# Input weights of a dense layer decoded ahead and parked in memory, with one scale to four chunks, and two transfers of a crossing issued in one step

## The chip, the cores and the metric

The kernel runs on one core of one Trainium2 chip. The metric is the device time of one execution in microseconds, from three runs of the kernel before; a separate profiled execution gives the trace. The engines are called TensorE (PE in the rows, PEld for its weight loads), VectorE (DVE), ScalarE (ACT), GpSimd (POOL) and SyncE (SP, here a queue of DMA issues).

## The reference, cut to what matters

```python
x = attention(q, k, v, w_pre, w_post)   # talking heads, 4 x 12 heads, 448 tokens, 64 wide
x = x.reshape(1792, 768)
a, b = x @ w1, x @ w2                    # 768 -> 1024
x = ((a * b) @ w3) @ w_out               # 1024 -> 1024 -> 768
h = x @ w_in                             # 768 -> 2048   (the input layer)
r = np.maximum(h, 0.0)
return (r * r) @ w_out2                  # 2048 -> 768   (the last stage)
```

All data is float32 in the reference; the weights arrive as float64 words, of which the kernel makes fp32 on the chip ("decode").

## The kernel before

Every fp32 factor is held as two fp16 halves, high and low, and each product is three matmuls (high x high, high x low, low x high). Halves need a common power of two as scale, which needs the largest magnitude over all 128 partitions. That is found by a *crossing*: a column of per-partition sums is stored to memory (`across`, L833), read back broadcast to all partitions (`ac`, L837), and reduced on DVE (`largest_sent`, L852), all DMAs issued from POOL; `pow2` (L109 to L114) makes the scale.

The work goes in stages: attention (to about 455 us); the first dense layer (columns `fc` 0 to 7, 144 matmuls each, `hidden_tile`); the product of `w3` and `w_out` into `M` (680 to 750); the x2 stage, `h @ M` over four strips of 448 tokens (750 to 860), each strip with a crossing of its own (`x2_steps`) before its halves are cast; the input layer (`layer_in`, eight pairs `p` of 128 output columns, 144 matmuls a pair, `in_tile`), whose results are squared on ACT (L1595, L1596) and stored (`g`); and the last stage, a product by a seven-multiplication scheme (L1715), whose weights `ow` are mixed from pairs of decoded output weights (`mixed_out`).

Weights come in *chunks* of 768 KB, in the order of the list `chunks`. One chunk's decode is ACT `Abs` (L799), DVE L800, L804, L807, ACT `Abs` with a sum (L811) and DVE L813. For `w1`, `w2` and `in`, two chunks make a pair: both are decoded, their sums `tot` cross together, and both are cast, the high half on ACT (L904), the low half on DVE (L907) (`pair_steps`). While the crossing is away, `between` decodes the chunk that follows if its kind allows it. An output chunk (`out`) is decoded and parked in memory as fp32 (`kept_out`), to be read again by `mixed_out`. Decoded chunks are in a ring of three tiles (`xa`), raw ones in a ring of two, cast weights in two rings of four (`w_tile`). The list after `M` is: in 0, in 1, out 0 to 7, in 2, in 3, out 8, out 9, in 4, in 5, and so on to out 15, then in 10 to in 15.

The order of instructions on the engines is written out while the program is built, by a planner. It has a clock `now`, which `tick` moves on as matmuls are written (1.13 for each two contraction steps, six matmuls), expected busy times of ACT, DVE and POOL, and streams of steps, each with an engine, a cost or a rest. A step is written when its engine is expected free within `ahead` and its rests are over; `GATE` holds a chunk until `allow[0]` has reached it. Where a result is asked for that is not written yet (`need`), its stream's steps are written at once, without rests. Streams cost nothing on the chip; they only place instructions in the engines' in-order queues. The lines on the crossing's wait in `pair_steps` are

```python
WAY = 14.0
...
yield REST, lambda: max(0.0, box["at"] + WAY + 3.0 - now[0]), None
yield DVE, 1.0, scale
...
yield REST, HAND, None
for k, z in ((0, 0), (1, 0), (0, 1), (1, 1)):
    yield (ACT, DVE)[z], 1.0, lambda k=k, z=z: cast(k, z)
```

In the x2 stage `allow[0]` is the place of out 7; in pair `p` of the input layer it is the place of in `2p + 3`.

Of the kernel before, what the change touches and what calls it, by code (L numbers as in the profile page):

```python
# [10 lines left out]
F32 = mybir.dt.float32  # L11
# [7 lines left out]
P = 128  # L19
# [16 lines left out]
def talking_heads_attention_moe_moe2(  # L36
# [675 lines left out]
            chunks += [("wl", f) for f in range(NFC // 2, NFC)]  # L712
        chunks.append(("w3", 4 * p + 2 * j + g))
    OG = NF2 // 2
    for p in range(NP2):
        chunks += [("in", 2 * p), ("in", 2 * p + 1)]
        if p == 0:
            chunks += [("out", j) for j in range(OG)]
        elif 2 * p + OG <= NF2:
            chunks += [("out", OG + 2 * p - 2), ("out", OG + 2 * p - 1)]  # L720
    place = {c: i for i, c in enumerate(chunks)}
    kept = {j: dram.tile([P, DM], F32, name=f"kept_{j}") for j in range(NFC // 2, NFC)}
    kept_out = [dram.tile([P, DM], F32, name=f"kept_out_{j}") for j in range(NF2)]
    out_sums = [sm.tile([P, OG], F32, tag="osum", name="osum", bufs=2) for _ in range(2)]
    wraw, wsp = {}, {}
# [97 lines left out]
    ncross = [0]  # L823
    ACT, DVE, POOL, REST, GATE = range(5)

    def crossing(src, n, box, wait):

        ncross[0] += 1
        d = dram.tile([P, n], F32, name=f"across_{ncross[0]}")
        w = 2 if n < 3 else n  # L830

        def there():
            nc.gpsimd.dma_start(d, src)  # L833

        def back():
            t = sm.tile([P, P * w], F32, tag=f"ac{w}", name="ac", bufs=4 // w)[:, : P * n]
            nc.gpsimd.dma_start(  # L837
                t, d.rearrange("p n -> (p n)").unsqueeze(0).to_broadcast([P, P * n])
            )
            box["sent"] = t  # L840

        yield after(wait)
        yield REST, 0.7, None
        yield POOL, 0, there
        yield REST, WAY / 2, None
        yield POOL, 0, back
        yield REST, WAY / 2, None
# [14 lines left out]
    def pair_steps(i, dma, between=None):  # L862
# [5 lines left out]
        n = 2  # L868

        def issue():  # L870
            box["way"] = Stream(crossing(tot, 2, box, ACT))
            streams.append(box["way"])
            box["at"] = now[0]

        def scale():
            finish(box["way"])
            box["scale"] = pow2(largest_sent(box.pop("sent"), n), 14, "ws", n)

        def turned():
# [53 lines left out]
        if between:  # L933
            yield from between(i + 2)
        if dma is not None:
            yield REST, lambda: max(0.0, box["at"] + WAY + 3.0 - now[0]), None
            yield DVE, 1.0, scale
        yield REST, HAND, None
        for k, z in ((0, 0), (1, 0), (0, 1), (1, 1)):
# [3 lines left out]

    def between(i):

        if i >= len(chunks) or chunks[i][0] not in ("wo", "in", "out", "w1") or i > allow[0]:
            return
        if chunks[i][0] == "out":
            return
        if chunks[i][0] == "wo":  # L950
            yield from one_steps(i)
            begun[i] = True
            return
        t1 = sm.tile([P, 1], F32, tag="t1", name="t1")
        load_to(i + 1)
        x, ops = decode(wraw.pop(i), DM, t1)

        def hand(total):
            nc.vector.tensor_copy(total, t1)
            return x  # L960

        yield from read_raw(i, x, ops)
        begun[i] = hand

    def one_steps(i):
        kind, j = chunks[i]
        load_to(i + 1)
        t = wraw.pop(i)
        if kind == "wl":
            load_to(i + 2)  # L970
            hh = wo_tiles(j)[0]
            yield ACT, 0.9, lambda: nc.scalar.copy(hh, t.bitcast(F32))

            def low():
                nc.vector.tensor_tensor(t, t.bitcast(F32), hh, op=ALU.subtract)
                wsp["wo", j] = wsp[chunks[i]] = (hh, t)

            yield DVE, 1.0, low
            return
        n = 4 * P if kind == "w3" else DM  # L980
        if kind == "out":
            x, ops = decode(t, n, out_sums[j // OG][:, j % OG : j % OG + 1])
            yield from read_raw(i, x, ops)
            yield POOL, 0, lambda: put_later(DVE, ("kept", j // OG), kept_out[j], x)
            wsp[kind, j] = True
            return
        x, ops = (decode_alone if kind == "w3" else decode)(t, n)
        yield from read_raw(i, x, ops)
        if kind == "w3":
            hh, ll = (  # L990
                pools["w"].tile([P, 4 * P], F32R, tag="wv"[z], name="w3", bufs=WB) for z in range(2)
            )
        elif j >= NFC // 2:
            yield POOL, 0, lambda: nc.sync.dma_start(kept[j], x)
            return
        else:
            hh, ll = wo_tiles(j)
        yield ACT, 0.9 * n / DM, lambda: nc.scalar.copy(hh, x)

        def low():  # L1000
            nc.gpsimd.tensor_tensor(ll, x, hh, op=ALU.subtract)
            wsp[kind, j] = (hh, ll)

        yield POOL, 2.0, low

    def load_to(n):
        while done[0] < min(n, limit[0]):
# [38 lines left out]

    def weight_steps(i):
        while i < len(chunks):
            if chunks[i][0] in ("w1", "in"):
                yield GATE, i + 1, None  # L1050
                yield from pair_steps(i, nc.gpsimd, between)
                i += 2
            else:
                if begun.pop(i, None) is None:
                    yield GATE, i, None
                    yield from one_steps(i)
                i += 1
# [13 lines left out]
                puts.remove(x)  # L1071

    def flush_kept():
        for g in range(2):
            flush(("kept", g))

    def tick(us, act=0.0, dve=0.0):
        flush(None, now[0])
# [10 lines left out]
    def finish(st):  # L1089
        while st.step(True) is not None:  # L1090
            pass
        if st in streams:
            streams.remove(st)
# [365 lines left out]
    xb = [sp.tile([P, NDC, NT], F16, tag="S", name="x2") for _ in range(2)]  # L1459
    x2 = [(xb[0][:, c], xb[1][:, c]) for c in range(NDC)]  # L1460

    allow[0] = place["out", OG - 1]

    def x2_steps(i, ts, xm):
        box = {}
# [10 lines left out]

    x2_done = []
    for i in range(B):
        xm = sm.tile([P, NDC + 1], F32, tag="xm", name="xm")
        ts = []  # L1480
        for c in range(NDC):
# [28 lines left out]
    def mixed_out(g):  # L1510
# [10 lines left out]

        def sides(q):
            bs = [w_tile(1, "ob").rearrange("p a d -> p (a d)").bitcast(F32) for _ in range(2)]
            flush(("kept", g))
            for z in range(2):
                nc.sync.dma_start(bs[z], kept_out[g * OG + 2 * q + z])
            box["b"] = bs
# [45 lines left out]
        return mixed[g]  # L1573

    def layer_in(p, gm):
        ws = [need(("in", 2 * p + j)) for j in range(2)]
        for st in x2_done[: B - 1]:
            finish(st)
        sc = [sm.tile([P, B], F32, tag=f"sci{j}", name="sci") for j in range(2)]
# [107 lines left out]

    gm = None
    for p in range(NP2):
        allow[0] = place["in", 2 * p + 3] if 2 * p + 4 < NF2 else len(chunks)  # L1690
        g, r = divmod(2 * p, OG)
        if r == 0:
            gm = sm.tile([P, OG, B], F32, tag="gm", name="gm")
        layer_in(p, gm)
        if r == OG - 2:
            g_scales[g] = Stream(g_scale(g, gm))
            streams.insert(0, g_scales[g])
        if p == 0:
            streams.append(mixed_out(0))
        elif p == NP2 - 1:  # L1700
            streams.append(mixed_out(1))
        if p == NP2 - 2:
            streams.append(tokens)
# [179 lines left out]
```

## Time and profile before

| | |
|---|---|
| median of three runs | 1371.28 us (1371.28 to 1372.92) |
| the profiled execution's own time | 1368.81 us |
| its span in the trace | 1367.0 us |
| mean granted TensorE clock | 0.969 |
| busy share PE, DVE, ACT, POOL | 92%, 68%, 56%, 39% |

The busy share is an average over stages. The granted clock is given as a share of 2.4 GHz. In a row of the timeline the brackets hold the engine's idle time before the instruction and what ended it.

### The profile page before, as it was taken

The numbers are of one execution on the slowest core, as the hardware profiler recorded it, in microseconds if no ns is written. First come the engines' busy times: TensorE is split into PE (matmuls) and PEld (weight loads), VectorE is DVE, ScalarE is ACT, GpSimd is POOL, SyncE is SP. The second block draws the span as 40 slices with busy tenths as digits, with TensorE's granted clock in tenths as the row PEclk, the third lists the DMA queues.
The fourth block names the chain that finished last, engine by engine and source line by source line (L and its number), as shares of the span: only waits on it lengthen the run. The fifth ranks groups of instructions, "written<-read, shape, count | busy, mean of one in ns | idle before, by whom it ended". The sixth has DMA issues, their size and how long they took to land. (4 is left out here: it accounts for less than half of the span.)

```text
span 1367.0 us, 26049 instructions
## 1 busy us (share of the span) xinstructions
PE 1254.2 (92%) x10022; PEld 760.5 (56%) x10022; DVE 932.2 (68%) x1758; ACT 759.5 (56%) x1502; POOL 531.3 (39%) x545
## 2 busy tenths in 40 slices
PE   8999999999999999888999999876586899999998
PEld 4666766766666555444599555432242344555565
DVE  6988898888898566655797565444653323699764
ACT  6878888788876344333443444445554545665330
POOL 4997788897794010000122000001400003577340
PEclk9999999999999999988999999998888999999999
DMA  6455455455567233232343245356735533555562
GB/s 190 131 159 154 131 158 153 125 162 157 141 173 205 53 104 89 74 85 85 105 150 108 51 79 168 66 110 188 217 109 145 133 106 123 177 157 184 158 198 93
DMA packets 130336, 182.99 MB, mean 134 GB/s; under 512 B 33348, under 2 KB 110788, under 8 KB 130212
## 3 DMA queue, kind: packets, MB, share of 16 engines
q1 hardware_dynamic: 125364, 176.41, 46.1%
q0 software_dynamic: 1712, 2.51, 1.3%
q10 hardware_dynamic: 3136, 2.40, 0.7%
q8 instruction: 79, 1.29, 0.4%
q14 instruction: 45, 0.37, 0.1%
HBM read 104.37 MB, written 38.38 MB: 104 GB/s over the span
## 5 line engine op out<-in xcount | busy, mean ns | idle before, releaser
L1106 PE MATMUL mm<-x,w 128*128 128x448 f16 x2196 | 437.8, 362 | 91.3 <-ACT w L904 72.3
L1106 PEld LDWEIGHTS <-w 128*128 128x128 f16 x2304 | 227.3, 100 | 320.5 <-ACT w L904 76.7
L1715 PE MATMUL mm<-ow,ao 128*128 128x384 f16 x1176 | 192.4, 326 | 6.1 <-DVE st L1731 5.6
L285 PE MATMUL p<-Bt,wpre_k 120*120 120x448 f32 x360 | 159.4, 560 | 5.1 <-DMA Bt<-S 4.9
L1715 PEld LDWEIGHTS <-ao 128*128 128x128 f16 x1176 | 115.0, 98 | 83.4 <-issue 7.7
L381 PEld LDWEIGHTS <-EH 120*112 120x112 f16 (+1 forms) x1440 | 124.7, 130 | 45.0 <-issue 37.2
L403 DVE TENSOR_TENSOR ATl<-o,ATh 112x480 f16<-112x480 f32 x180 | 116.1, 645 | 25.3 <-ACT ATh L397 24.6
L354 POOL TENSOR_SCALAR EH<-E,st 120x448 f16<-120x448 f32 (+1 forms) x152 | 115.7, 769 | 43.7 <-DVE st L337 32.7
L307 ACT ACTIVATE E<-p,st 120x448 f32<-120x448 f32 x180 | 116.1, 645 | 22.9 <-DVE st L299 13.6
L381 PE MATMUL o<-wph,EH 120*112 120x120 f16 x720 | 123.9, 219 | 1.8 <-DVE ATl L403 0.9
L397 ACT CAST ATh<-o 112x480 f16<-112x480 f32 x180 | 101.2, 562 | 43.1 <-PE o L381 38.1
L381 PE MATMUL o<-wph,EL 120*112 120x120 f16 x720 | 122.0, 216 | 0.0
L381 PE MATMUL o<-wpl,EH 120*112 120x120 f16 x720 | 122.0, 216 | 0.0
L366 POOL TENSOR_TENSOR EL<-F,EH 120x448 f16<-120x448 f32 (+1 forms) x90 | 103.2, 1146 | 34.9 <-issue 21.2
L833 POOL DMA_DIRECT2D across<-tot x15 | 8.4, 562 | 276.7 <-ACT xa L811 276.7
L299 DVE TENSOR_REDUCE st<-p 120x1 f32<-120x448 f32 x180 | 110.2, 613 | 2.4 <-PE p L285 2.2
L1106 PE MATMUL mm<-h,M 128*128 128x448 f16 x576 | 109.8, 353 | 0.8 <-ACT M L1284 0.6
L381 PEld LDWEIGHTS <-EL 120*112 120x112 f16 x720 | 93.6, 130 | 0.0
L368 DVE SCALAR_TENSOR_TENSOR EL<-E,st,EH 120x448 f16<-120x448 f32 (+1 forms) x90 | 83.1, 923 | 10.2 <-POOL EH L354 9.7
L811 ACT ACTIVATE xa<-xa 128x768 f32<-128x768 f32 x54 | 45.4, 840 | 75.4 <-DVE xa L807 68.9
L1106 PEld LDWEIGHTS <-M 128*128 128x128 f16 x576 | 55.9, 98 | 53.9 <-DVE M L1280 1.9
L249 ACT COPY S<-s 110x896 f32<-110x896 f32 (+1 forms) x88 | 80.5, 914 | 8.7 <-PE s L242 7.7
(232 smaller groups left out, 2219.5 us busy)
## 6 DMA issues: line engine op xcount, KB each, us to landing
Bt<-S SPq DMA_DIRECT2D x176, 210.0 KB
raw<-in_moe_w_out_dram SPq DMA_DIRECT2D x24, 768.0 KB
g<-st SPq DMA_DIRECT2D x64, 224.0 KB
gt<-g SPq DMA_DIRECT2D x56, 256.0 KB
raw<-in_moe_w_in_dram SPq DMA_DIRECT2D x16, 768.0 KB
raw<-in_moe_w_dram SPq DMA_DIRECT2D x14, 768.0 KB
raw<-in_moe_w_dram SPq DMA_DIRECT2D x16, 512.0 KB
kept_out<-xa SPq DMA_DIRECT2D x16, 384.0 KB
```

The source lines that it names most:

```text
L249: nc.scalar.copy(Stile[s][:R, 2 * p : 2 * p + 2, :], Ps.pop((s, p))[:R, :, :S])
L285: nc.tensor.matmul(pt[: n * H, :S], wpre_k.rearrange("p t g -> p (t g)")[: n * H, : n * H], Bt.pop(u)[: n * H], start=True, stop=True,)
L299: nc.vector.tensor_reduce(nsum[u][:n, 0, j : j + 1], Pp[u][:n, :S], axis=AX.X, op=ALU.max, negate=True)
L307: nc.scalar.activation(e[:n], Pp.pop(u)[:n, :S].rearrange("p (a b) -> p a b", a=EG), AF.Exp, bias=t[:n, 0, j : j + 1], scale=1.0, accum_ou ...
L354: nc.gpsimd.tensor_scalar(seven(EH[u][:n]), Ex[u][:n], inverse(u), 1.0, op0=ALU.mult, op1=ALU.mult)
L366: nc.gpsimd.tensor_tensor(a, f, b, op=ALU.subtract)
L368: nc.vector.scalar_tensor_tensor(a, e, inverse(u), b, op0=ALU.mult, op1=ALU.subtract)
L381: nc.tensor.matmul(pt[:CP, c * n : (c + 1) * n], a[:n, c * CP : (c + 1) * CP], w[:n, :n], start=(i == 0), stop=(i == 2),)
L397: nc.scalar.copy(ATs[s][0][:, :, :, m * NR : m * NR + nr], src)
L403: nc.vector.tensor_tensor(ATs[s][1][:, :, :, a], src, ATs[s][0][:, :, :, a], op=ALU.subtract)
L1106: nc.tensor.matmul(pt[:, :S], w[a][:, cs], x[z][:, sl], start=(c == 0 and i == 0), stop=(c == len(parts) - 1 and i == 2),)
L1715: nc.tensor.matmul(pt[:, :OH], y[:, a, q * P : (q + 1) * P], ow[g, q][:, w, kb], start=(start and q == 0 and m == 0), stop=(q == NQ - 1 an ...
```

## The change

Input chunks are no longer handled as pairs. Each is decoded by itself (`one_steps`), its sum goes to a column of `in_sums`, and its fp32 form is parked in memory (`kept_in`). When the fourth of a group is decoded, a stream `cast_in` starts: one crossing for the four, one scale, and then pair by pair a reload of two chunks from memory (tiles `ib` of ring 1, issued on SP) and their casts. A pair is let go when `layer_in` has begun the pair before it (`pair_now`); pairs 0 and 1 are let go in the x2 stage. The list after `M` becomes in 0 to 7, out 0 to 3, in 8 to 11, out 4, out 5, in 12 to 15, out 6 to 15, and `allow[0]` lets three chunks go in each strip of the x2 stage and in each pair of the input layer. The parked stores have one key for all, so any flush issues all of them.

For `w1` and `w2`, the pair's crossing becomes `send`: both DMAs are written on POOL at once, with no step in between; the scale's step rests 14 from there and not 17.

```diff
--- before.py
+++ after.py
@@ -712,14 +712,13 @@
             chunks += [("wl", f) for f in range(NFC // 2, NFC)]
         chunks.append(("w3", 4 * p + 2 * j + g))
     OG = NF2 // 2
-    for p in range(NP2):
-        chunks += [("in", 2 * p), ("in", 2 * p + 1)]
-        if p == 0:
-            chunks += [("out", j) for j in range(OG)]
-        elif 2 * p + OG <= NF2:
-            chunks += [("out", OG + 2 * p - 2), ("out", OG + 2 * p - 1)]
+    LAST = ["in"] * 8 + ["out"] * 4 + ["in"] * 4 + ["out"] * 2 + ["in"] * 4 + ["out"] * 10
+    chunks += [(k, LAST[:i].count(k)) for i, k in enumerate(LAST)]
     place = {c: i for i, c in enumerate(chunks)}
     kept = {j: dram.tile([P, DM], F32, name=f"kept_{j}") for j in range(NFC // 2, NFC)}
+    IG = 4
+    kept_in = [dram.tile([P, DM], F32, name=f"kept_in_{j}") for j in range(NF2)]
+    in_sums = sm.tile([P, NF2], F32, tag="isum", name="isum", bufs=1)
     kept_out = [dram.tile([P, DM], F32, name=f"kept_out_{j}") for j in range(NF2)]
     out_sums = [sm.tile([P, OG], F32, tag="osum", name="osum", bufs=2) for _ in range(2)]
     wraw, wsp = {}, {}
@@ -823,6 +822,18 @@
     ncross = [0]
     ACT, DVE, POOL, REST, GATE = range(5)
 
+    def send(src, n, dma):
+
+        ncross[0] += 1
+        d = dram.tile([P, n], F32, name=f"across_{ncross[0]}")
+        dma.dma_start(d, src)
+        w = 2 if n < 3 else n
+        t = sm.tile([P, P * w], F32, tag=f"ac{w}", name="ac", bufs=4 // w)[:, : P * n]
+        dma.dma_start(
+            t, d.rearrange("p n -> (p n)").unsqueeze(0).to_broadcast([P, P * n])
+        )
+        return t
+
     def crossing(src, n, box, wait):
 
         ncross[0] += 1
@@ -868,12 +879,10 @@
         n = 2
 
         def issue():
-            box["way"] = Stream(crossing(tot, 2, box, ACT))
-            streams.append(box["way"])
+            box["sent"] = send(tot, 2, dma)
             box["at"] = now[0]
 
         def scale():
-            finish(box["way"])
             box["scale"] = pow2(largest_sent(box.pop("sent"), n), 14, "ws", n)
 
         def turned():
@@ -933,7 +942,7 @@
         if between:
             yield from between(i + 2)
         if dma is not None:
-            yield REST, lambda: max(0.0, box["at"] + WAY + 3.0 - now[0]), None
+            yield REST, lambda: max(0.0, box["at"] + WAY - now[0]), None
             yield DVE, 1.0, scale
         yield REST, HAND, None
         for k, z in ((0, 0), (1, 0), (0, 1), (1, 1)):
@@ -943,9 +952,7 @@
 
     def between(i):
 
-        if i >= len(chunks) or chunks[i][0] not in ("wo", "in", "out", "w1") or i > allow[0]:
-            return
-        if chunks[i][0] == "out":
+        if i >= len(chunks) or chunks[i][0] not in ("wo", "w1") or i > allow[0]:
             return
         if chunks[i][0] == "wo":
             yield from one_steps(i)
@@ -978,11 +985,16 @@
             yield DVE, 1.0, low
             return
         n = 4 * P if kind == "w3" else DM
-        if kind == "out":
-            x, ops = decode(t, n, out_sums[j // OG][:, j % OG : j % OG + 1])
+        if kind in ("in", "out"):
+            sums = in_sums[:, j : j + 1] if kind == "in" else out_sums[j // OG][:, j % OG : j % OG + 1]
+            x, ops = decode(t, n, sums)
             yield from read_raw(i, x, ops)
-            yield POOL, 0, lambda: put_later(DVE, ("kept", j // OG), kept_out[j], x)
-            wsp[kind, j] = True
+            yield POOL, 0, lambda: put_later(DVE, "kept", (kept_in if kind == "in" else kept_out)[j], x)
+            if kind == "in" and j % IG == IG - 1:
+                streams.append(Stream(cast_in(j // IG)))
+                casts.append(streams[-1])
+            elif kind == "out":
+                wsp[kind, j] = True
             return
         x, ops = (decode_alone if kind == "w3" else decode)(t, n)
         yield from read_raw(i, x, ops)
@@ -1002,6 +1014,51 @@
             wsp[kind, j] = (hh, ll)
 
         yield POOL, 2.0, low
+
+    casts, pair_now = [], [-1]
+
+    def cast_in(g):
+
+        box = {}
+        a = sm.tile([P, 1], F32, tag="im", name="im")
+
+        def top():
+            nc.vector.tensor_reduce(a, in_sums[:, g * IG : (g + 1) * IG], axis=AX.X, op=ALU.max)
+
+        def scale():
+            box["scale"] = pow2(largest_sent(box.pop("sent"), 1), 14, "is")
+
+        def sides(q):
+            box["b"] = [
+                w_tile(1, "ib").rearrange("p a d -> p (a d)").bitcast(F32)[:, :DM] for _ in range(2)
+            ]
+            flush("kept")
+            for z in range(2):
+                nc.sync.dma_start(box["b"][z], kept_in[2 * q + z])
+
+        yield after(ACT)
+        yield DVE, 0.3, top
+        yield from crossing(a, 1, box, DVE)
+        yield DVE, 0.8, scale
+        up, lo = box["scale"]
+        for q in range(g * IG // 2, (g + 1) * IG // 2):
+            while q > pair_now[0] + 1:
+                yield REST, 0.5, None
+            yield POOL, 0, lambda: sides(q)
+            yield REST, 5.0, None
+            for z in range(2):
+                x, w = box["b"][z], w_tile(0)
+                yield ACT, 0.95, lambda: nc.scalar.activation(w[:, 0], x, AF.Copy, scale=up)
+                yield DVE, 1.0, lambda: nc.vector.scalar_tensor_tensor(
+                    w[:, 1], x, up, w[:, 0], op0=ALU.mult, op1=ALU.subtract
+                )
+                wsp["in", 2 * q + z] = (w, lo)
+
+    def need_in(j):
+        while ("in", j) not in wsp:
+            st = casts[j // IG] if j // IG < len(casts) else weights
+            assert st.step(True)
+        return wsp["in", j]
 
     def load_to(n):
         while done[0] < min(n, limit[0]):
@@ -1046,7 +1103,7 @@
 
     def weight_steps(i):
         while i < len(chunks):
-            if chunks[i][0] in ("w1", "in"):
+            if chunks[i][0] == "w1":
                 yield GATE, i + 1, None
                 yield from pair_steps(i, nc.gpsimd, between)
                 i += 2
@@ -1071,8 +1128,7 @@
                 puts.remove(x)
 
     def flush_kept():
-        for g in range(2):
-            flush(("kept", g))
+        flush("kept")
 
     def tick(us, act=0.0, dve=0.0):
         flush(None, now[0])
@@ -1459,7 +1515,8 @@
     xb = [sp.tile([P, NDC, NT], F16, tag="S", name="x2") for _ in range(2)]
     x2 = [(xb[0][:, c], xb[1][:, c]) for c in range(NDC)]
 
-    allow[0] = place["out", OG - 1]
+    pair_now[0] = 0
+    after_m = place["in", 0]
 
     def x2_steps(i, ts, xm):
         box = {}
@@ -1476,6 +1533,7 @@
 
     x2_done = []
     for i in range(B):
+        allow[0] = after_m + 3 * i + 2
         xm = sm.tile([P, NDC + 1], F32, tag="xm", name="xm")
         ts = []
         for c in range(NDC):
@@ -1521,7 +1579,7 @@
 
         def sides(q):
             bs = [w_tile(1, "ob").rearrange("p a d -> p (a d)").bitcast(F32) for _ in range(2)]
-            flush(("kept", g))
+            flush("kept")
             for z in range(2):
                 nc.sync.dma_start(bs[z], kept_out[g * OG + 2 * q + z])
             box["b"] = bs
@@ -1573,7 +1631,8 @@
         return mixed[g]
 
     def layer_in(p, gm):
-        ws = [need(("in", 2 * p + j)) for j in range(2)]
+        pair_now[0] = p
+        ws = [need_in(2 * p + j) for j in range(2)]
         for st in x2_done[: B - 1]:
             finish(st)
         sc = [sm.tile([P, B], F32, tag=f"sci{j}", name="sci") for j in range(2)]
@@ -1687,7 +1746,7 @@
 
     gm = None
     for p in range(NP2):
-        allow[0] = place["in", 2 * p + 3] if 2 * p + 4 < NF2 else len(chunks)
+        allow[0] = min(after_m + 3 * (p + B) + 2, len(chunks))
         g, r = divmod(2 * p, OG)
         if r == 0:
             gm = sm.tile([P, OG, B], F32, tag="gm", name="gm")
```

## Rows read from the trace of the kernel before

**Rows 1.** Page, busy time: engine, us (share), instructions; weight loads behind it.

```profile
PE 1254.2 (92%) x10022; PEld 760.5 (56%) x10022; DVE 932.2 (68%) x1758; ACT 759.5 (56%) x1502; POOL 531.3 (39%) x545
```

**Rows 2.** Windows by stage: length, busy us of each engine, granted clock, DMA share, GB/s.

```profile
456.00:680.00 224.00, 205.33 (x1045) 103.04 (x1044) 144.86 (x283) 84.19 (x130) 16.68 (x19) 0.95 0.31 80
...
750.00:860.00 110.00, 109.67 (x579) 56.33 (x580) 64.87 (x127) 46.75 (x83) 3.84 (x7) 1.00 0.41 103
860.00:1165.00 305.00, 232.34 (x1156) 114.37 (x1155) 129.96 (x220) 153.73 (x306) 42.65 (x44) 0.89 0.49 131
1165.00:1367.00 202.00, 192.21 (x1176) 114.80 (x1174) 149.47 (x190) 88.26 (x138) 100.90 (x69) 1.00 0.54 162
```

**Rows 3.** Waits, 860 to 1165 us: total us, times, longest.

```profile
PE mm L1106 <- ACT w L904: 58.1, 7, 19.6
...
PE mm L1106 <- ACT x L1284: 11.8, 2, 8.4
...
PE mm L1106 <- DVE w L907: 2.0, 4, 0.5
```

**Rows 4.** Timeline of TensorE, 855 to 1170 us: start, length, instructions, idle before.

```profile
860.17 6.97 PE L1106 MATMUL mm<-x,w 128*128 128x448 f16 x36
...
906.27 27.04 PE L1106 MATMUL mm<-x,w 128*128 128x448 f16 x142 [0.50 <-DVE w L907]
945.67 0.93 PE L1106 MATMUL mm<-x,w 128*128 128x448 f16 x2 [12.37 <-ACT w L904]
...
996.15 29.35 PE L1106 MATMUL mm<-x,w 128*128 128x448 f16 x144 [19.60 <-ACT w L904]
...
1164.82 5.36 PE L1715 MATMUL mm<-ow,ao 128*128 128x384 f16 x32
```

**Rows 5.** Timeline of POOL, DVE and ACT, 925 to 948 us.

```profile
930.69 0.55 POOL L833 DMA_DIRECT2D across<-tot  x1 [10.83 <-ACT xa L811]
...
942.73 0.42 DVE L852 TENSOR_REDUCE acr<-ac 128x2 f32<-128x256 f32 x1 [10.38 <-DMA ac<-across]
...
944.68 1.76 ACT L904 ACTIVATE w<-xa,ws 128x768 f16<-128x768 f32 x2 [9.39 <-DVE ws L114]
```

**Rows 6.** Timeline of TensorE, 456 to 690 us.

```profile
465.54 81.89 PE L1106 MATMUL mm<-x,w 128*128 128x448 f16 x432 [2.05 <-DVE w L907]
549.49 27.04 PE L1106 MATMUL mm<-x,w 128*128 128x448 f16 x142 [2.05 <-DVE w L907]
581.14 30.33 PE L1106 MATMUL mm<-x,w 128*128 128x448 f16 x144 [4.62 <-ACT w L904]
616.43 29.76 PE L1106 MATMUL mm<-x,w 128*128 128x448 f16 x144 [4.96 <-ACT w L904]
650.80 29.64 PE L1106 MATMUL mm<-x,w 128*128 128x448 f16 x144 [4.61 <-ACT w L904]
680.12 10.21 PE L1353 MATMUL mm<-wo,w 128*128 128x384 f32 x57
```

**Rows 7.** Timeline of SP and ACT, 966 to 984 us.

```profile
969.30 1.54 SPq L1526 DMA_DIRECT2D ob<-kept_out  x2
...
976.87 0.94 ACT L1565 ACTIVATE ow<-ob,os 128x768 f16<-128x768 f32 x1 [0.35 <-DMA ob<-kept_out]
```

**Rows 8.** Timeline of DVE, 853 to 876 us.

```profile
868.64 0.29 DVE L852 TENSOR_REDUCE acr<-ac 128x1 f32<-128x128 f32 x1 [11.67 <-DMA ac<-across]
```

**Rows 9.** Timeline of ACT and DVE, 590 to 618 us.

```profile
594.81 0.61 ACT L1148 ACTIVATE st<-mm,sc 128x448 f32<-128x448 f32 x1
595.33 0.90 ACT L799 ACTIVATE zt<-raw 128x768 f32<-128x768 f32 x1
...
614.19 0.41 DVE L852 TENSOR_REDUCE acr<-ac 128x2 f32<-128x256 f32 x1
```

**Rows 10.** Timeline of POOL, 870 to 1120 us.

```profile
909.70 0.55 POOL L833 DMA_DIRECT2D across<-om  x1 [13.38 <-DVE om L1517]
...
992.55 0.99 POOL L1530 TENSOR_TENSOR ot<-ob,ot 128x384 f32<-128x384 f32 x1
```

## The prediction

> **What bounds the kernel now.** I read the page's busy table first: TensorE is busy 92% of the span [rows 1], so time can only come out of the 8% in which it stands still and out of stretches at a lower clock. Then the windows by stage [rows 2]: the granted clock is 0.95 in the first dense layer (456 to 680 us), 1.00 in the x2 stage and in the last stage, and 0.89 in the input layer (860 to 1165 us), a mean between the levels of 2.4 and 1.2 GHz; TensorE lacks 73 us of work in the last of these and about 19 us in the first. So I asked who it waited for [rows 3]: in the input layer 58.1 us for the high part of a weight (ACT, L904), 2.0 us for its low part, 11.8 us for the x2 operand.
>
> The timeline of TensorE [rows 4] gives the rate of a full-clock stretch, 142 matmuls in 27.04 us, 190.4 ns each. The input layer has 8 pairs x 144 = 1152 matmuls, 219.4 us at that rate; it takes 860.17 to 1164.82, 304.7 us. The loss is 85.3 us: the waits of rows 3 (72.3 with small ones of x2) and 13 us of slower matmuls behind them (after the 19.60 us wait 144 matmuls took 29.35 us and not 27.42).
>
> What is late there [rows 5]: the second chunk's sum reaches POOL at 930.69, the crossing through memory comes back to DVE at 942.73, ACT casts at 944.68, and TensorE, out of work, starts the pair after 12.37 us. Decode of a pair, crossing and cast do not fit into the 27 us that the pair before lasts, because in the list of chunks two output chunks stand ahead of each pair.
>
> In the first dense layer [rows 6] the seven columns after the first take from about 463.5 to 680.1, 216.6 us; at full rate 1008 matmuls are 191.9, so 24.7 us are lost: waits of 2.05, 2.05, 4.62, 4.96, 4.61 and 7.5 us of slow matmuls behind the last three (30.33 + 29.76 + 29.64 against 3 x 27.42).
>
> **The change, part by part: the input weights.** Removed: 8 crossings of a pair, of which the first was already hidden and seven are behind the waits. Added: 4 crossings of a group of four, 16 stores and 16 reloads of 393 KB, the same 16 decodes and 16 casts. What counts is when a pair can be cast. Groups 0 and 1 are decoded in the x2 stage, three chunks to a strip. Chunk 11, the last of group 2, is let go in pair 1 and due in pair 4; chunk 15 is let go in pair 3 and due in pair 6. So each scale has two pairs, 54.8 us, of spare, where the crossing needs 12 us [rows 5]. What remains at the time of use is reload and cast, let go one pair ahead: a comparable reload of two tiles of 393 KB was issued at 969.30 and its second cast, which waited for it, ran at 976.87 [rows 7], so 7.6 us; two casts on ACT take 1.76 us (944.68) and DVE's low parts about as long again, so some 12 of 27.4 us. The load on the engines fits: in the input layer ACT was busy 153.7 and DVE 130.0 us [rows 2]; with 20 chunks decoded there in place of 22 (by the two lists) that is still under 219. SP gets two reloads a pair; traffic was 131 GB/s over 305 us, 40 MB at a DMA share of 0.49; 12 more stores and 12 reloads of 0.393 MB less two loads of 0.786 make it 48, in 219 us a share of 0.82, full but not over.
>
> So the weight waits go, 58.1 + 2.0, with their part of the slow matmuls. Of the 85.3 us, x2 keeps 12.2 of waits and, for two waits, twice the 1.9 us of slow matmuls behind the 19.60 us wait, 16.0 together; the weight part is 69.3. Below it is bounded by 0 (the waits come back at the reload), above by 69.3. I take 65.3, because 4 us for eight small handovers like the 0.50 us of 906.27 are likely to stay.
>
> **The x2 stage** gets 12 decodes where it had 10, two more casts, and four reloads. TensorE has no waits in it now, but DVE runs late: the strip's scale was waited for 11.67 us up to 868.64 with later reductions behind it [rows 8], and that sets the waits at x2, 11.8 us [rows 3]. DVE was busy 64.9 us there [rows 2]; if all of that were the ten decodes, two more would be 13 us, and a third of it, 4 us, I add to the x2 waits, as the halving of x2 and the reductions are in it too. Bounds: -16.0 (DVE less late, as the chunks are now let go strip by strip) to +13.
>
> **The first dense layer.** Only the crossing changes: both transfers go out at once, and the scale is let go 14 and not 17 planner microseconds after. The planner counts 1.13 for six matmuls, 27.12 for a column of 144. In column 5 the issue stands between ACT's eviction at 594.81 and the next decode at 595.33 [rows 9], that is after the third tile: 9 ticks, 10.17. Adding 17 gives 27.17, just past the end, so the step is only forced when the next column asks; that agrees with DVE's order, where the scale (614.19) stands behind the whole end of the column. Cast and TensorE's start at 616.43 follow it. Adding 14 gives 24.17: the scale is let go at the 22nd tick and the casts at the 23rd, before the last tile's DVE work, while the crossing has landed (it can start once the eviction of 594.81 is past, and took 12 us in rows 5). So the three long waits go: 4.62 + 4.96 + 4.61 and 7.5 of clock, 21.7. The two of 2.05 I leave in; 20.6 is what the 24.7 leaves beside them, and I take that. Bounds 0 and 24.7. POOL is now held while the first transfer lands, a part of the 12 us, and the low part of an output weight queues behind it; that is due only after 680, so it costs nothing.
>
> The Trainium skill (DMA: Bandwidth & Descriptors, Anatomy of one DMA) says that a semaphore wait is served by the issuing sequencer before dispatch, so a reload that must wait for its parking store holds everything behind it on SP. By that rule the time would be the second rival's, 1322, where the rows give 1289; no row of before has such a reload of input weights.
>
> The last stage starts with its operands as before: the first output mix now starts in pair 4 and not in pair 1; from its crossing to its last subtraction it took 909.70 to 992.55 [rows 10], 83 us, in which TensorE waited about 32 [rows 4], while pairs 4 to 7 are 110 us. I cost it at nothing; if it is not done, the last stage's start waits, which is in the range.
>
> **Sum.** The profiled execution took 1368.8 us (span 1367.0), 2.5 under the median 1371.3. 1368.8 - 65.3 - 20.6 + 4 = 1286.9; against the median, 1289.
>
> **The rivals.**
> 1. The first layer's scale still comes behind the column's end (the margin in planner time is one tick on either side): 1289 + 20.6 = 1310. Against it: the arithmetic on rows 9. Chance 0.12.
> 2. SP is held by reloads behind parking stores, raw chunks come late, and decode falls behind again. A hold as long as the reload of rows 7, 7.6 us for 8 pairs, is 61 us against the spare of 54.8, so only the last groups run dry; half of the 65.3 back is 1322. For it: SP carries all stores and loads. Against it: store and reload lie a crossing apart, 12 us. Chance 0.12.
> 3. Slower: a cast on ACT that waits for its reload holds the evictions behind it. TensorE has eight banks of 18 matmuls, 27.4 us, before it stops. It decides from a reload of 27.4 us; at 40 us for eight pairs it costs 101, 1390. Against it: 7.6 us in rows 7. Chance 0.06.
> 4. No gain: each pair is asked for before it was let go, and casts are forced at the column as now: 1371. Against it: the spare of two pairs. Chance 0.04.
> 5. x2 too is in time, as its strips are no longer behind ten chunks in a row: 1289 - 4 - 16 = 1269. Chance 0.08.
> 6. The forecast, 1289; own range 1272 to 1304 from the bounds of its small terms. Chance 0.58.
>
> **Range and chances.** 1264 to 1324 takes in cases 1, 2, 5 and 6 with their bounds and leaves out the rest and the far ends. Changes within 0.2%, 2.7 us, are about what a measurement of this kernel cannot tell from none. Faster 0.90 (1, 2, 5, 6), same 0.04 (4), slower 0.06 (3).
>
> **What would show it.** TensorE's waits for ACT L904 in the input layer near zero, the granted clock there above 0.97, the stage 235 us long from its first matmul to the last stage's; DVE's scale in columns 5 to 7 of the first layer ahead of the last tile's reduction; no waits over 1 us between columns. It is wrong if TensorE waits for casts of reloaded tiles, if the x2 waits grow past 25 us, or if the last stage starts with a wait for the first mix.

## The result, and the profile after

The changed kernel takes 1269.49 us (median of four runs, 1268.77 to 1271.91) against 1371.28: a ratio of 0.926, interval 0.924 to 0.928. The forecast was 1289 with a range of 1264 to 1324. The profiled execution took 1268.8 us, its span is 1267.1 us, and the mean granted clock rose from 0.969 to 0.994.

Line numbers have moved: the product of the dense layers is L1162 (was L1106), the pair's casts L913 and L916 (L904 and L907), the scale's reduction L863 (L852), the x2 operand on ACT L1340 (L1284). New are the casts of reloaded input weights, L1051 on ACT and L1052 on DVE, and their reload, L1037.

The page's busy table of the changed kernel, to set beside [rows 1]:

```profile
PE 1236.4 (98%) x10022; PEld 760.4 (60%) x10022; DVE 928.2 (73%) x1742; ACT 757.9 (60%) x1502; POOL 527.0 (42%) x537
```

TensorE's share went from 92% to 98%. Its busy time fell by 18 us with the same 10022 instructions: those are the matmuls that ran slower after each wait. The windows by stage, as in [rows 2], with one stretch of 27 us at the end:

```profile
455.00:652.00 197.00, 197.00 (x1044) 101.91 (x1042) 145.45 (x283) 84.58 (x130) 17.68 (x19) 1.00 0.37 91
...
723.00:833.00 110.00, 109.66 (x579) 56.30 (x580) 71.09 (x141) 49.46 (x87) 6.01 (x10) 1.00 0.58 136
833.00:1065.00 232.00, 220.89 (x1156) 113.29 (x1155) 118.71 (x191) 149.22 (x302) 37.61 (x33) 0.98 0.74 208
1065.00:1267.00 202.00, 192.19 (x1176) 114.80 (x1174) 149.85 (x190) 88.31 (x138) 101.14 (x69) 1.00 0.54 162
943.00:970.00 27.00, 27.00 (x144) 13.99 (x143) 5.04 (x15) 10.74 (x24) 2.17 (x4) 1.00 0.99 174
```

The timeline of TensorE from the first dense layer on, to set beside [rows 4] and [rows 6]:

```profile
455.03 197.65 PE L1162 MATMUL mm<-x,w 128*128 128x448 f16 x1044
...
833.18 20.59 PE L1162 MATMUL mm<-x,w 128*128 128x448 f16 x108
863.26 0.53 PE L1162 MATMUL mm<-x,w 128*128 128x448 f16 x1 [9.48 <-ACT x L1340]
863.98 151.45 PE L1162 MATMUL mm<-x,w 128*128 128x448 f16 x791 [0.19 <-DVE x L1336]
1015.91 6.97 PE L1162 MATMUL mm<-x,w 128*128 128x448 f16 x36 [0.48 <-ACT st L1654]
1023.84 41.13 PE L1162 MATMUL mm<-x,w 128*128 128x448 f16 x216 [0.96 <-ACT st L1654]
1064.81 56.71 PE L1774 MATMUL mm<-ow,ao 128*128 128x384 f16 x348
```

And the waits of TensorE from 430 us to the end, as in [rows 3]:

```profile
PE mm L1162 <- ACT x L1340: 9.5, 1, 9.5
PE mm L1774 <- DVE st L1790: 5.7, 5, 1.7
PE mm L1162 <- ACT st L1654: 1.4, 2, 1.0
```

No wait for a weight of either dense layer is left. The first layer is a single line of 1044 matmuls without a gap; the input layer has one wait for the x2 operand and two short ones for an eviction, a kind of wait that this layer did not have before. Stage by stage, from first matmul to first matmul of the next: the first dense layer went from 223.98 to 197.33 us (-26.65), the input layer from 304.65 (1164.82 - 860.17) to 231.63 (-73.0); everything else together changed by -0.2. The sum is -99.9, the difference of the spans.

### The profile page after: what moved, and what is told of

It is laid out like the page before. It is cut to its first block, busy times and chain, and to the rows that moved or that the text cites. A ratio compares the mean times of both kernels' runs of the same rounds, so it can differ in the third digit from the quotient of the medians.

```text
span 1267.1 us, 26092 instructions
## 1 busy us (share of the span) xinstructions
PE 1236.4 (98%) x10022; PEld 760.4 (60%) x10022; DVE 928.2 (73%) x1742; ACT 757.9 (60%) x1502; POOL 527.0 (42%) x537
## 4 chain that ended last, share of the span: by engine, by line
PE 70%; DMA 11%; DVE 8%; issue 4%; ACT 4%; POOL 2%; SPq 1%; ACTq 0%; POOLq 0%; DVEq 0%
PE mm L1162 25%; PE mm L1774 11%; PE p L285 10%; PE o L381 8%; PE s L242 5%; PE a L495 5%; PE mm L1409 4%; DMA raw<-in_moe_w_out_dram 2%; DMA Bt<-S 2%; PE p L1162 2%; DMA kept_out<-xa 2%; DMA raw<-in_moe_w_in_dram 1%; DVE ow L1626 1%; DMA g<-st 1%; DMA ob<-kept_out 1%
## 5 line engine op out<-in xcount | busy, mean ns | idle before, releaser
L1162 PE MATMUL mm<-x,w 128*128 128x448 f16 x2196 | 418.3, 353 | 11.1 <-ACT x L1340 9.5
L1162 PEld LDWEIGHTS <-w 128*128 128x128 f16 x2304 | 225.3, 98 | 222.9 <-issue 14.3
L1162 PE MATMUL mm<-h,M 128*128 128x448 f16 x576 | 109.8, 353 | 0.8 <-ACT M L1340 0.6
L368 DVE SCALAR_TENSOR_TENSOR EL<-E,st,EH 120x448 f16<-120x448 f32 (+1 forms) x90 | 83.1, 923 | 10.8 <-POOL EH L354 10.4
L1162 PEld LDWEIGHTS <-M 128*128 128x128 f16 x576 | 55.9, 98 | 53.9 <-DVE M L1336 1.9
L285 PEld LDWEIGHTS p<-Bt,wpre_k 120*120 120x120 f32 x360 | 57.5, 183 | 47.8 <-issue 19.3
```

Of the source, the lines that this page charges most:

```text
L285: nc.tensor.matmul(pt[: n * H, :S], wpre_k.rearrange("p t g -> p (t g)")[: n * H, : n * H], Bt.pop(u)[: n * H], start=True, stop=True,)
L368: nc.vector.scalar_tensor_tensor(a, e, inverse(u), b, op0=ALU.mult, op1=ALU.subtract)
L1162: nc.tensor.matmul(pt[:, :S], w[a][:, cs], x[z][:, sl], start=(c == 0 and i == 0), stop=(c == len(parts) - 1 and i == 2),)
```

## The experiments

The letters in the texts on record: for the first layer, A says that the place of the scale's step in the engines' order makes the gain, B that it is the issue of both transfers in one step. For the input layer, C says that the lead makes it, that is the order of the chunks with their gates, which has the weights decoded before they are asked for. D is C's rival and differs by run: in e9 that the input layer waits for the crossing itself, in e4 that fewer crossings make the gain (four and not eight), in e6 that parking with a separate cast makes it. Each ratio in the table is to the kernel before, run beside that run.

| run | median us | ratio, interval |
|---|---|---|
| e1: step let go 3 us later | 1297.85 | 0.946, 0.943 to 0.950 |
| e2: old two-step transfers | 1269.75 | 0.926, 0.923 to 0.929 |
| e3: before, with the edit of the first layer alone | 1343.64 | 0.980, 0.976 to 0.984 |
| e9: before, with that edit for all pairs | 1329.49 | 0.970, 0.966 to 0.973 |
| e4: groups of two | 1274.74 | 0.928, 0.926 to 0.930 |
| e6: groups of two, order of before | 1367.27 | 0.997, 0.995 to 0.998 |
| e5: no lead for reload and cast | 1316.08 | 0.959, 0.957 to 0.961 |
| e7: x2 stage's chunks let go at once | 1284.99 | 0.937, 0.935 to 0.939 |
| e8: last x2 scale through TensorE | 1263.69 | 0.924, 0.921 to 0.927 |
| e10: e8, second step later | 1263.19 | 0.923, 0.920 to 0.925 |
| e11: the changed kernel once more, beside e10 | 1269.41 | 0.927, 0.924 to 0.929 |

### The first dense layer: e1 and e2

e1 is the changed kernel with the old distance between crossing and scale:

```diff
-            yield REST, lambda: max(0.0, box["at"] + WAY - now[0]), None
+            yield REST, lambda: max(0.0, box["at"] + WAY + 3.0 - now[0]), None
```

> The changed kernel with the scale of a pair of w1 and w2 let go 17 planner microseconds after the issue, as before, and both transfers still going out at once. Theory A (the place of the scale's step in the engines' order makes the gain of the first dense layer): the scale falls behind the end of the column again and most of the 26.7 us that the first layer gained are lost, 1290 (1284 to 1296). Theory B (the transfers themselves, out at once, make it): 1269.5 within 3.

e2 keeps the new distance and takes the transfers back to two steps:

```diff
-            box["sent"] = send(tot, 2, dma)
+            box["way"] = Stream(crossing(tot, 2, box, ACT))
+            streams.append(box["way"])
...
+            finish(box["way"])
```

> The changed kernel with the crossing of a pair of w1 and w2 again in two steps with rests between, and the scale let go 14 after the issue. Theory A: the gain of the first layer stays but for what a later second transfer costs, 1270 to 1276. Theory B: it is lost, 1290 to 1296.

The two came out 28 us apart. The timeline of TensorE in e1, columns 5 to 7:

```profile
583.75 30.01 PE L1162 MATMUL mm<-x,w 128*128 128x448 f16 x144 [4.61 <-ACT w L913]
618.73 29.60 PE L1162 MATMUL mm<-x,w 128*128 128x448 f16 x144 [4.96 <-ACT w L913]
652.93 0.55 PE L1162 MATMUL mm<-x,w 128*128 128x448 f16 x2 [4.61 <-ACT w L913]
```

These are the waits of [rows 6] to within 0.01 us, and the two of 2.05 us came back too. The time lies a little above A's 1284 to 1296: the layer took 226.8 us, 2.8 more than in the kernel before. In e2 the whole layer is one line again:

```profile
454.42 197.65 PE L1164 MATMUL mm<-x,w 128*128 128x448 f16 x1044
```

So A holds and B fell: issuing the transfers together is worth nothing here, letting the scale go three planner microseconds earlier is worth 28 us. The timeline of DVE at the end of a column shows how (L1207 evicts a tile of results, L1180 takes its maximum, L1369 closes the column). In the changed kernel:

```profile
572.67 0.42 DVE L863 TENSOR_REDUCE acr<-ac 128x2 f32<-128x256 f32 x1 [3.63 <-DMA ac<-across]
...
573.82 0.68 DVE L1207 SCALAR_TENSOR_TENSOR st<-mm,sc,st 128x448 f32<-128x448 f32 x1
574.54 0.62 DVE L1180 TENSOR_REDUCE hm<-st 128x1 f32<-128x448 f32 x1
...
576.93 0.15 DVE L1369 TENSOR_REDUCE hm<-hm 128x1 f32<-128x4 f32 x1
```

In e1:

```profile
579.25 0.68 DVE L1207 SCALAR_TENSOR_TENSOR st<-mm,sc,st 128x448 f32<-128x448 f32 x1 [5.47 <-PE mm L1162]
579.97 0.62 DVE L1180 TENSOR_REDUCE hm<-st 128x1 f32<-128x448 f32 x1
580.62 0.16 DVE L1369 TENSOR_REDUCE hm<-hm 128x1 f32<-128x4 f32 x1
...
581.51 0.41 DVE L863 TENSOR_REDUCE acr<-ac 128x2 f32<-128x256 f32 x1
```

In e1 the scale (L863) stands behind the last tile's reduction (L1180) and the column's closing work, which need TensorE's last matmul; so the next column's cast can't start before this column ends. It waits for no transfer there. In the changed kernel it stands ahead of the last tile's work; DVE waits 3.63 us for the crossing, and nobody waits for DVE.

### Parts on the kernel before: e3 and e9

e3 puts the one-step transfer and the distance of 14 into the kernel before for the first layer's pairs (kind "w1") only; e9 drops that condition, so the input layer's pairs get it too.

```diff
-            box["way"] = Stream(crossing(tot, 2, box, ACT))
-            streams.append(box["way"])
+            if kind == "w1":
+                box["sent"] = send(tot, 2, dma)
+            else:
+                box["way"] = Stream(crossing(tot, 2, box, ACT))
+                streams.append(box["way"])
...
-            yield REST, lambda: max(0.0, box["at"] + WAY + 3.0 - now[0]), None
+            yield REST, lambda: max(0.0, box["at"] + WAY + (0.0 if kind == "w1" else 3.0) - now[0]), None
```

> The kernel before with the change of the first dense layer alone (both transfers at once, rest 14, for w1 and w2 only). If the two parts add up, the first layer takes 197 us as in the changed kernel and the input layer 305 as before: 1371.3 - 26.7 = 1344.6. If part of the gain of the first layer came from the input weights' part (through the order of later steps), the time is 1350 or more.

> The kernel before with both transfers at once and rest 14 for all pairs, those of the input weights too. Theory C (the input layer is short of lead: two output chunks stand ahead of each pair): the waits there fall by little, as the planner asks for each pair before it is ready anyway, 3 us for each of seven waits at most, 1325 to 1345. Rival D (the crossing is what the input layer waits for): the waits fall by more than half, below 1315.

e3 is 27.6 us under before, the size that e1 lost, and its input layer waits as before (59.0 us in seven waits for the high part of a weight, where [rows 3] has 58.1). The two halves of the change add up: 1343.6, less the 73.0 of the input layer, is 1270.6. e9 wins 14 us more; its waits for a weight are 13.44, 16.87, 12.85 and 6.04 us, and the last pairs run on without one. So the one-step transfer and the shorter distance together bring a fifth of what the input layer had to give; C's 1325 to 1345 held and D's time below 1315 was not reached. Which of the two brings it no run tells.

### The input weights: e4, e6 and e5

e4 shares a scale among two chunks in place of four: eight crossings, everything else as changed. e6 adds the chunk order and the gates of before.

```diff
-    IG = 4
+    IG = 2
```

> The changed kernel with groups of two chunks in place of four: eight crossings and eight scales for the input weights, all else the same (lead, order, parking). Theory C (lead): 1269.5 within 4, as each scale still has at least one pair of spare. Rival D (fewer crossings make the gain): half of the 69 us or more come back, 1300 or more.

e6 beside that:

```diff
-    LAST = ["in"] * 8 + ["out"] * 4 + ["in"] * 4 + ["out"] * 2 + ["in"] * 4 + ["out"] * 10
+    LAST = ["in"] * 2 + ["out"] * 8 + (["in"] * 2 + ["out"] * 2) * 4 + ["in"] * 6
...
-        allow[0] = after_m + 3 * i + 2
+        allow[0] = place["out", OG - 1]
...
-        allow[0] = min(after_m + 3 * (p + B) + 2, len(chunks))
+        allow[0] = place["in", 2 * p + 3] if 2 * p + 4 < NF2 else len(chunks)
```

> The changed kernel with input weights parked and cast in pairs from memory, but with the chunks in the order of the kernel before, its gates, and a scale for each pair. Theory C: the waits of the input layer come back, and with the reload behind each crossing they are longer than before; 1345 is the kernel before with the first layer's gain, so 1345 to 1400. Rival D: parking with a separate cast makes the gain, under 1300.

e4 has no wait for a weight. It is 5 us slower, a little more than the 4 that C allowed, with waits at x2 of 16.2 us (two) against 9.5; the intervals of the two ratios overlap. D fell: the number of crossings is not the gain. In e6 the waits of TensorE in the input layer are

```profile
PE mm L1162 <- ACT w L1051: 82.7, 7, 21.9
```

more than the 58.1 us of [rows 3]; in that order a reload now stands between the crossing and the cast as well. So parking does not make the gain: e6 stands at 1367.3 against 1343.6 of e3, which has the old order, eight crossings and no parking (e6 also decodes each chunk by itself, so the 24 us are the price of both). What wins, with parking in place, is the order of the chunks and their gates, 92.5 us between e6 and e4; between e3 and e4 it is 69. No run has the new order without parking.

e5 keeps the order and takes away the one pair by which reload and cast are let go ahead:

```diff
-            while q > pair_now[0] + 1:
+            while q > pair_now[0]:
```

> The changed kernel with a pair's reload and cast let go only when its own turn begins, not one pair before. By the sum of the prediction reload and cast take 12 us, for seven pairs (pair 0 stays ahead) 84 us, and some 2 us of slower matmuls behind each, 98 together: 1367. If the reload is quicker when nothing else runs, 8 us and 2 us each, 1340.

It came out at 1316, under both expectations. The timeline of TensorE shows waits from 2.25 to 11.12 us, among them:

```profile
906.22 29.22 PE L1162 MATMUL mm<-x,w 128*128 128x448 f16 x144 [5.14 <-ACT w L1051]
...
976.90 29.72 PE L1162 MATMUL mm<-x,w 128*128 128x448 f16 x144 [11.12 <-ACT w L1051]
1017.57 29.86 PE L1162 MATMUL mm<-x,w 128*128 128x448 f16 x144 [10.95 <-ACT w L1051]
```

Seven waits sum to 38.0 us, 5.4 each and not 12; with slower matmuls behind them the input layer is some 50 us longer (831.33 to 1112.77). The lead of one pair is worth 47 us. The 5.4 us are what TensorE waits, and not what reload and cast take. The timeline of SP, ACT and DVE in e5, ahead of the matmuls at 906.22:

```profile
897.18 3.88 SPq L1037 DMA_DIRECT2D ib<-kept_in  x2
...
905.23 1.98 ACT L1051 ACTIVATE w<-ib,is 128x768 f16<-128x768 f32 x2 [2.78 <-DMA ib<-kept_in]
...
906.20 2.06 DVE L1052 SCALAR_TENSOR_TENSOR w<-ib,is,w 128x768 f16<-128x768 f32 x2 [4.58 <-ACT w L1051]
```

The reload goes out 3.9 us before TensorE runs dry (901.08), and TensorE starts again before the last casts are done. From the reload's issue to the end of the low parts are 11.1 us here, 8.0 to 17.1 over the seven pairs and 10.9 in the mean, so the 12 of the prediction were near. What the expectation had wrong was to count all of it as a wait: in six of the seven pairs the reload was out 3.5 to 7.1 us before TensorE ran dry.

### The x2 operand: e7, e8, e10

e7 lets the x2 stage's twelve chunks go from its first strip on and not three to a strip:

```diff
-        allow[0] = after_m + 3 * i + 2
+        allow[0] = after_m + 3 * B - 1
```

> The changed kernel with all twelve chunks of the x2 stage allowed from its start, not three a strip. Theory: the pacing keeps DVE less late and makes x2's waits fall from 11.8 to 9.5 us; without it the last two strips are late again, 1272 to 1280. Rival: the planner paces itself by its own costs, and nothing changes, 1269.5 within 3.

The timeline of TensorE in e7, end of the x2 stage and start of the input layer:

```profile
837.02 8.65 PE L1162 MATMUL mm<-x,w 128*128 128x448 f16 x36 [2.81 <-DVE xm L1180]
853.40 0.53 PE L1162 MATMUL mm<-x,w 128*128 128x448 f16 x1 [7.73 <-ACT x L1340]
...
878.42 0.53 PE L1162 MATMUL mm<-x,w 128*128 128x448 f16 x1 [8.44 <-ACT x L1340]
```

Both x2 waits of before are back, and the reductions on DVE now hold TensorE's banks as well (4.3 us in three waits). The direction was expected; the size, 15.5 us, lies outside the 1272 to 1280 on record. So with twelve chunks the order in which decodes are let go sets how late DVE is. That the pacing took away one of the two waits of before does not follow: e6 and e9 let ten chunks go at once, as the kernel before, and have one x2 wait each (8.8 and 9.8 us), while e4 is paced and has two (16.2).

The other, 9.48 us, stayed. The timeline of DVE, POOL and ACT in the changed kernel, last strip:

```profile
843.00 0.16 DVE L1551 TENSOR_REDUCE xm<-xm 128x1 f32<-128x6 f32 x1
...
843.45 1.02 POOL L844 DMA_DIRECT2D across<-xm  x1 [16.98 <-DVE sci L1641]
...
852.41 0.54 POOL L848 DMA_DIRECT2D ac<-across  x1 [7.94 <-DMA across<-xm]
...
856.82 0.56 DVE L799 TENSOR_SCALAR xa<-raw 128x768 int32<-128x768 int32 x1 [5.62 <-DMA raw<-in_moe_w_in_dram]
...
861.12 0.28 DVE L863 TENSOR_REDUCE acr<-ac 128x1 f32<-128x128 f32 x1
...
862.56 2.33 ACT L1340 ACTIVATE x<-st,xs 128x448 f16<-128x448 f32 x4
```

From the maximum (843.00) to the scale (861.12) there are 18.1 us: the store took until 852.4, the reload and a decode that itself waited 5.62 us for its raw chunk the rest. e8 takes this strip's maximum past memory: a transpose and a product with ones on TensorE.

```diff
...
+        if i == B - 1:
+            yield REST, 9.0, None
+            yield POOL, 0, turned
+            yield DVE, 0.25, top
+            yield REST, 2.0, None
+            yield POOL, 0, spread
+            yield DVE, 1.1, scale_ps
...
```

> The changed kernel, with the maximum over partitions of the last x2 strip taken by a transpose and a small matmul on TensorE in place of the crossing through memory. If the 17 us of that crossing (843.5 to 861) are what the remaining wait of 9.48 us at x2 is for, the wait goes with the slower matmuls behind it, some 11 us: 1258 to 1262. If DVE, late by ten microseconds at the end of the x2 stage, is the limit, the wait becomes one of TensorE for the transpose or for DVE, and the time stays within 4 of 1269.5.

The wait at x2 is gone, and a part of it came back inside the new path, so that the time lies between the two on record. On TensorE's timeline:

```profile
848.49 0.58 PE L1538 MATMUL mm<-acr,ones 1*128 1x1 f32 x2 [4.80 <-DVE acr L1534]
```

The second product stands in TensorE's order before DVE has got to the reduction that it needs. e10 puts it later (the second REST 7.0):

> As the run before (the last x2 strip's maximum taken on TensorE), with the small matmul that spreads it placed some two tiles later in TensorE's order. If the 4.8 us that TensorE waited there are only a matter of the place (DVE's reduction came behind two decodes), they go: 4 to 5 us less than the run before, 1258 to 1260. If x2 is then late itself, the wait moves to the first tile of the last strip, 1262 to 1265.

The waits of TensorE in e10:

```profile
PE mm L1162 <- ACT x L1340: 1.8, 1, 1.8
PE mm L1538 <- DVE acr L1534: 1.7, 1, 1.7
```

The wait was spread and not removed, and the time stayed, inside the second of its two ranges (1262 to 1265). e11, run beside e10, is the changed kernel again:

> The changed kernel itself, beside the run above on the same chip, for the comparison: 1269.5 within 3.

e10 is 6.2 us under it. The intervals of the two ratios overlap (0.9203 to 0.9252, 0.9241 to 0.9292), so that half per cent is likely rather than sure; the spans, 1261.6 and 1267.4, differ by as much, about what the shorter waits explain (9.5 against 3.5).

## Why the prediction was right, point by point

The mechanism was right in both layers, and the sum was 18 us high against the profiled execution (1286.9 against 1268.8): 6.0 in the first layer, 11.7 in the input layer, 0.2 elsewhere. The time lies within the stated range of 1264 to 1324, but 2.5 us below the forecast's own 1272 to 1304.

**First dense layer.** Predicted -20.6, measured -26.65, beyond the bound of 24.7. The planner arithmetic held: the scale stands ahead of the last tile's reduction at a distance of 14 and behind the column's end at 17. The term was mis-sized by leaving in the two waits of 2.05 us, for which I had no cause; e1 shows that they hang on the same three microseconds. The other 2 us were lost in the sum: the waits and slow matmuls listed for the 24.7 add up to 25.8, and the full rate is 189.3 ns over the 1044 matmuls in a line, not 190.4. Rival 1 fell, and the one-step transfer that I had tied to this term adds nothing (e2).

**Input weights.** Predicted -65.3 of a weight part of 69.3. The 4 us for small handovers did not stay: no wait for a cast is left. What came in their place is 1.4 us of waits for an eviction. The stage's loss against full rate went from 85.3 to 12.2 us (231.63 - 219.4), of which 9.7 are x2's waits and 1.4 the evictions'. So of the 11.7 us that the sum was high here, 4 are the handovers and at least 9.2 the x2 term, less the 1.4. The weight part is thus gone as the spare of two pairs had it, with the reason confirmed by e4 and e6: lead, not fewer crossings. Of the inputs to that step, reload and cast took 10.9 us in the mean of e5's seven pairs, near the 12; and the bytes were as estimated (208 GB/s over 232 us are 48 MB), with a DMA share of 0.74 over the stage (estimate 0.82), but 0.99 in the 27 us from 943 on.

**x2.** Here the step failed in its sign: I added 4 us, and the x2 part of the loss fell from 16.0 to 10.8 at the most. DVE did get more work in the stage (71.1 against 64.9 us, near the half of the 13 I had bounded it by), but it was less late. The last strip's maximum came 15.4 us after the input layer's first matmul (860.17) in the kernel before, on DVE's timeline

```profile
875.52 0.16 DVE L1493 TENSOR_REDUCE xm<-xm 128x1 f32<-128x6 f32 x1
```

and 9.8 us after it in the changed one (843.00 against 833.18). The pacing strip by strip, rival 5's mechanism, with a chance of 0.08, is shown to matter for twelve chunks (e7). It is not shown to be what made DVE less late than before: in e9 and e6, with ten chunks let go at once, the same maximum came 7.2 and 11.4 us after (839.22 and 844.99 against 831.99 and 833.58). That cause stays open. Rival 5's time, 1269, was met by luck: only one of its two waits went, and the rest of the way came from the first layer and from the handovers.

**Rivals 2 and 3** showed themselves without deciding. The timeline of SP and ACT at the fullest stretch, and of ACT 35 us later:

```profile
946.70 11.96 SPq L1127 DMA_DIRECT2D g<-st  x3
958.87 1.66 SPq L1037 DMA_DIRECT2D ib<-kept_in  x2
...
971.36 1.81 ACT L1051 ACTIVATE w<-ib,is 128x768 f16<-128x768 f32 x2 [6.35 <-DMA ib<-kept_in]
...
1010.85 0.94 ACT L1623 ACTIVATE ow<-ot,os 128x768 f16<-128x768 f32 x1 [3.25 <-POOL ot L1588]
1014.41 0.93 ACT L1623 ACTIVATE ow<-ot,os 128x768 f16<-128x768 f32 x1 [2.63 <-POOL ot L1588]
1015.25 0.61 ACT L1654 ACTIVATE st<-mm,sci 128x448 f32<-128x448 f32 x1
```

On SP the reload stands behind three stores of evicted strips, a row of 11.96 us. The issues themselves are short (0.66, 0.32 and 0.32 us, at 946.70, 950.91 and 958.33); between them the queue stood, and its own waits from 943 to 962 us begin with

```profile
SPq L1127 <- DMA kept_out<-xa: 7.0, 1, 7.0
SPq L1127 <- DMA raw<-in_moe_w_out_dram: 3.5, 1, 3.5
```

By the trace the longest part is thus a strip's store that stood until the parking store of an output chunk had landed; why it depends on that no run shows. From the reload's own issue to its first cast are 12.5 us, where [rows 7] had 7.6 to the second. That is a hold on SP of rival 2's size, with another head than the reload behind its parking store that the Trainium skill (DMA: Bandwidth & Descriptors, Anatomy of one DMA) led me to; ahead of a reload of input weights it came once, and it made no weight late. ACT then fell behind through waits at casts, first this one, later output weights that waited for POOL, and with the last of these the banks ran out: the next eviction is at 1015.25 and TensorE resumes at 1015.91 after 0.48 us, and 0.96 us were lost once more. So rival 3's mechanism was met at its edge, through the sum of several waits and not one reload of 27 us, for 1.4 us and not 101. At 3.41 us a tile (18 matmuls at 189.3 ns, an estimate) TensorE finished 17 tiles from 957.58, when ACT last waited for it, to 1015.4, and ACT had evicted 9 of them: eight stood in the banks. That is read from the trace; no run took the backlog away.

**What I had costed at nothing** cost nothing: POOL's hold during the transfers shows in no wait of TensorE, and the last stage starts without one (1064.81), so the first mix, three pairs later, was in time. The granted clock in the input layer is 0.98 (above the 0.97 named), the stage 231.6 us (235 named).

**Open:** how much of the last strip's 18.1 us is the crossing itself under the traffic and how much DVE's place behind a decode that waits for raw data; e8 avoided both at once.

## What to carry to other kernels

When a dependent chain is short of time, first ask whether it is let go early enough in each in-order engine: moving one step by three planner microseconds was worth 28 us and, with the weights parked, decoding ahead in another order 92, while transfers issued together were worth nothing and fewer crossings 5 us at most, not clear of the noise. Parking in memory in the old order cost (24 us here, with the handling of single chunks); it paid where the new order let the decode run ahead of the time of use, and reload and cast need their own lead as well (47 us here). After a wait is gone look at the engines that now carry waiting casts ahead of evictions: here their backlog was seen first as waits of TensorE for an eviction, 1.4 us.

## What the hardware showed that I had not expected

A crossing through memory is slow: the 128-element store of one strip's maximum needed 7.94 us after POOL had issued it (843.45 to 852.41), and 18.1 us passed to the scale; in [rows 5] a crossing took 12 us in all. The parking of the input weights is not the main reason: from issue to landing the four strips' stores (0.5 KB) took 8.1 us in the median in the kernel before and 9.2 in the changed one.

The DMA share and the rate of bytes part company: from 943 to 970 us the engines were 0.99 busy at 174 GB/s, while over the whole stage a share of 0.74 moved 208 GB/s. A full share here meant fewer bytes, not more, and two reloads issued in that stretch took 12.5 us to their first cast, where before two took 7.6. Why the stretch moved fewer bytes no run shows.
